# Second PV ahead of the transposes, an earlier v load, chosen PSUM tiles for the first FFN1 work, and no visit behind f0

## The chip, the cores and the metric

One core of one Trainium2 chip runs the whole kernel. The time is device microseconds (us) of an execution. An execution reads some 1.8 us more than the span of its profile (before: 417.85 us timed, 416.07 us span). Every comparison below is between fast-state runs, unless it says otherwise. "Granted clock" is the TensorE clock in the profile, 1.00 being full speed. Its records begin with the first stretch at full clock; what runs before that counts as 1.00 in the views and in the mean, whatever its speed.

## The reference

```python
scores = (1/sqrt(64)) * q @ k.T - log(448)        # q, k, v: 8 batches x 12 heads x 448 x 64
attn   = 1 / (1 + exp(-scores))                   # sigmoid, no softmax: tiles are independent
x      = (attn @ v) laid out as 3584 tokens x 768
g      = x @ w_gate                               # 768 x 1536
h      = g * sigmoid(g) * (x @ w_val)
out    = h @ w_out                                # 1536 x 768
```

## The kernel before

The work comes in quads: four heads of one batch, so 24 quads, three to a batch. A quad has 7 score tiles. Each is written by TensorE (four concurrent 64x64 products), goes through the sigmoid on ScalarE, and is used by the PV product of the quad; three PVs make one batch's input of FFN1. FFN1 of a batch is 12 tiles, f0 to f11, of 12 matmuls each: six for the gate, six for the value. In the views `st` is a loaded q or k, `c` its cast, `T` or `Tk` the transposed one, `pt` a sigmoid's output, `xT` the input of FFN1, and `s`, `t`, `hT` are the three steps from an FFN1 tile to h (sigmoid of the gate, then two products). Everything that TensorE writes goes through a ring of four PSUM tiles of two banks:

```python
ring = [psD.tile([128, 2, 512], FP32, tag=f"D{i}", name=f"ps_D{i}") for i in range(4)]
# Banked(): the next tile of the ring; Banked(at=i): a chosen one, the ring does not move on
def chunk(n, c):
    sig_tile(n, c, qk_tile(n, c))          # scores of tile c of quad n, then its sigmoid
```

The start, before FFN1 can run at full speed (GpSimd's loads, then the part of the program order that matters):

```python
    load_v(0)
    ... # casts of quad 1
    w_load("g", 0)
    load_v(1)
    w_load("v", 0)
    load_v(2)
    ...
    chunk(1, 5)
    chunk(1, 6)
    trans_pe(3)                            # 14 transposes on TensorE into one ring tile, two copies on VectorE
    for c in range(3):
        chunk(2, c)
    pv(1)
    ...
    chunk(2, 3)
    chunk(2, 4)
    # then FFN1 tiles f0..f2 of batch 0, cut up by chunk(2, 5), chunk(2, 6) and pv(2)
```

After the start, a list of units (FFN1 tiles, sums, output tiles) is run in order. A "visit" puts three or four score tiles of a later quad between two units when an estimated clock says so; the PV of the quad that is complete goes into the next visit.

```python
    for dur, fn, args in units:
        if vi < len(visits) and tcur >= vtime[vi]:
            ... # the visit
        fn(*args)
        tcur += dur
```

Tile f0 is issued in two parts (four input pairs, then two), because the last third of its input comes from the PV just ahead of it. The k and q of quads 6 and later are loaded to a staging tile by GpSimd's queue, cast there, and transposed by a DMA of SyncE.

## Time and profile before

| | before |
|---|---|
| time, median of 3 | 417.59 us (417.5 to 417.6) |
| span of the profile, mean clock | 416.1 us, 1.00 |
| TensorE busy | 403.6 us |
| first sigmoid, fourteenth sigmoid | 6.77, 18.47 us |
| second PV, FFN1, third PV | 20.52, 23.01, 27.16 us |
| first matmul of tile f3 of batch 0 | 32.65 us |
| from there to the end | 383.42 us |

The prediction below shows the main views. One that it doesn't show is the list of TensorE's waits: what waited, for what, us in total, how often, and the longest. Two of its rows belong to the change:

```profile
PE ps_D L198 <- ACT pt L246: 2.2, 3, 1.2
...
PE ps_D L294 <- DVE t L314: 0.4, 2, 0.2
```

The first is the transposes in the start. The second is the tile after f0, waiting for VectorE's read of f0, in two batches. I measure a stall differently in this document: as the time from one matmul's start to the next one's, over the median for the same pair of lines. Then these two are 0.29 us each (at 167.9 and 232.3 us). A third of 0.30 at 332.0 is inside a visit behind f0.

### The profile page before, as it was taken

The numbers are of one execution on the slowest core, as the hardware profiler recorded it, in microseconds if no ns is written. First come the engines' busy times: TensorE is split into PE (matmuls) and PEld (weight loads), VectorE is DVE, ScalarE is ACT, GpSimd is POOL, SyncE is SP. The second block draws the span as 40 slices with busy tenths as digits, with TensorE's granted clock in tenths as the row PEclk, the third lists the DMA queues.
The fourth block names the chain that finished last, engine by engine and source line by source line (L and its number), as shares of the span: only waits on it lengthen the run. The fifth ranks groups of instructions, "written<-read, shape, count | busy, mean of one in ns | idle before, by whom it ended". The sixth has DMA issues, their size and how long they took to land.

```text
span 416.1 us, 7945 instructions
## 1 busy us (share of the span) xinstructions
PE 403.6 (97%) x3194; PEld 210.7 (51%) x3194; DVE 257.2 (62%) x472; ACT 213.5 (51%) x294; POOL 94.6 (23%) x125
## 2 busy tenths in 40 slices
PE   7699999999999999999999999999999999999995
PEld 3444544445555445445565445445555545555563
DVE  3727647679855555668654555568745447588653
ACT  5966885745454745755704945745715562222000
POOL 4528063336030463110030335300000000000000
PEclk9999999999999999999999999999999999999999
DMA  8999999976779995331274998630025400000135
GB/s 254 253 253 244 226 185 236 187 184 172 189 131 241 187 195 166 71 107 24 55 190 134 201 165 191 144 57 0 2 63 137 112 2 0 2 0 2 38 80 148
DMA packets 59845, 54.39 MB, mean 131 GB/s; under 512 B 35744, under 2 KB 53280, under 8 KB 59808
## 3 DMA queue, kind: packets, MB, share of 16 engines
q0 software_dynamic: 18880, 30.94, 34.7%
q1 hardware_dynamic: 40496, 22.62, 24.9%
q8 instruction: 25, 0.41, 0.4%
q10 hardware_dynamic: 432, 0.33, 0.3%
q14 instruction: 12, 0.10, 0.1%
HBM read 47.19 MB, written 11.01 MB: 140 GB/s over the span
## 4 chain that ended last, share of the span: by engine, by line
PE 88%; ACT 5%; DVE 3%; DMA 1%; issue 1%; SPq 0%; DVEq 0%; ACTq 0%
PE ps_D L294 50%; PE ps_D L418 18%; PE ps_D L228 7%; PE ps_D L260 7%; PE ps_D L476 5%; ACT pt L246 3%; DMA st<-in_k_dram 1%; DVE t L314 1%; PE ps_D L198 1%; ACT s L312 1%; DVE S L377 1%; ACT pt L243 1%; DVE xT L269 0%; DVE hT L318 0%; DVE xT L274 0%
## 5 line engine op out<-in xcount | busy, mean ns | idle before, releaser
L246 ACT ACTIVATE pt<-ps_D,sb_t 128x896 f16<-128x896 f32 x148 | 140.3, 1011 | 82.0 <-PE ps_D L228 76.6
L294 PE MATMUL ps_D<-xT,wg 128*128 128x448 f16 x576 | 126.9, 353 | 1.1 <-ACT pt L246 0.5
L294 PE MATMUL ps_D<-xT,wv 128*128 128x448 f16 x576 | 126.5, 353 | 0.0
L314 DVE TENSOR_TENSOR t<-ps_D,s 128x448 f16<-128x448 f32 x96 | 59.8, 623 | 75.7 <-ACT s L312 75.3
L312 ACT ACTIVATE s<-ps_D 128x448 f16<-128x448 f32 x96 | 52.6, 548 | 85.2 <-PE ps_D L294 73.2
L294 PEld LDWEIGHTS <-wg 128*128 128x128 f16 x576 | 53.5, 98 | 59.2 <-issue 13.7
L294 PEld LDWEIGHTS <-wv 128*128 128x128 f16 x576 | 56.3, 98 | 52.9 <-issue 0.3
L179 POOL CAST c<-st 128x896 bf16<-128x896 f32 x41 | 38.2, 941 | 127.3 <-DMA T<-c 63.8
L318 DVE SCALAR_TENSOR_TENSOR hT<-ps_D,t 128x448 f16<-128x448 f32 x96 | 60.0, 625 | 10.0
L228 PE MATMUL ps_D<-T,T 64*64 64x448 bf16 x644 | 44.2, 357 | 1.4 <-DVE T L204 0.6
L260 PE MATMUL ps_D<-pt,v 64*64 64x448 f16 x672 | 36.0, 350 | 0.4 <-ACT pt L246 0.3
L429 DVE TENSOR_SCALAR osb<-ps_D 128x384 f32<-128x384 f32 x43 | 24.0, 558 | 19.1 <-PE ps_D L418 18.1
L418 PEld LDWEIGHTS <-S 128*128 128x128 f16 x264 | 25.8, 98 | 17.1
L418 PE MATMUL ps_D<-wT,S 128*128 128x384 f16 x198 | 34.0, 327 | 0.0
L228 PEld LDWEIGHTS <-T 64*64 64x64 bf16 x644 | 15.2, 105 | 23.8 <-issue 18.2
L269 DVE CAST xT<-ps_D 128x448 f16<-128x448 f32 x24 | 15.0, 623 | 19.9 <-PE ps_D L260 14.5
L435 DVE SCALAR_TENSOR_TENSOR osb<-ps_D,osb 128x384 f32<-128x384 f32 x33 | 18.4, 558 | 13.5 <-PE ps_D L418 13.5
L172 POOL DMA_DIRECT2D v<-in_v_dram x24 | 17.5, 730 | 39.9 <-PE ps_D L228 35.3
L274 DVE CAST xT<-ps_D 64x448 f16<-64x448 f32 x42 | 26.1, 621 | 0.7
L260 PEld LDWEIGHTS <-v 64*64 64x64 f16 x672 | 19.8, 107 | 13.1 <-issue 1.1
L418 PEld LDWEIGHTS <-hT 128*128 128x128 f16 x198 | 18.9, 98 | 14.2 <-issue 2.1
L476 PE MATMUL ps_D<-wo,hT 128*128 128x384 f16 x144 | 24.2, 327 | 0.3 <-DVE osb L489 0.3
(45 smaller groups left out, 211.6 us busy)
## 6 DMA issues: line engine op xcount, KB each, us to landing
out_dram<-osb SPq DMA_DIRECT2D x52, 192.0 KB, 2.9
st<-in_q_dram POOLq DMA_DIRECT2D x20, 448.0 KB, 5.0
st<-in_k_dram POOLq DMA_DIRECT2D x20, 448.0 KB, 6.4
v<-in_v_dram POOLq DMA_DIRECT2D x24, 224.0 KB, 7.7
wg<-in_moe_w_gate_dram POOLq DMA_DIRECT2D x4, 576.0 KB, 11.9
wv<-in_moe_w_val_dram POOLq DMA_DIRECT2D x4, 576.0 KB, 13.3
wo<-in_moe_w_out_dram POOLq DMA_DIRECT2D x4, 576.0 KB, 10.0
st<-in_q_dram SPq DMA_DIRECT2D x3, 448.0 KB, 7.1
```

Of the source, the lines that this page charges most:

```text
L179: eng.tensor_copy(out=t.rearrange("p c h d -> p h c d"), in_=st.rearrange("p h (c d) -> p h c d", c=C))
L228: nc.tensor.matmul(out=sc[w * 64:(w + 1) * 64, h2, :S], lhsT=kt[r, w * 64:(w + 1) * 64], rhs=qt[r, :, w * 64:(w + 1) * 64], start=True, st ...
L246: nc.scalar.activation(out=pt, in_=sc[:, :, :S], func=SIGM, bias=sb_t, scale=qkscale)
L260: nc.tensor.matmul(out=P[g:g + 64, h2, :S], lhsT=vt[r, h2, c * D:(c + 1) * D], rhs=pt[r, h2, :], start=(c == 0), stop=(c == C - 1),)
L274: done = [nc.vector.tensor_copy(out=o, in_=i) for o, i in halves[how:]]
L294: nc.tensor.matmul(out=D.t[:, i, :S], lhsT=w16[f // FW][:, pr, cs], rhs=xT[(b, pr)], start=(pr == 0), stop=(pr == NP - 1),),
L312: D.read(nc.scalar.activation(out=s16, in_=D.t[:, 0, :S], func=SIGM), 0)
L314: D.read(nc.vector.tensor_tensor(out=t1, in0=D.t[:, 0, :S], in1=s16, op=MULT), 0)
L318: nc.vector.scalar_tensor_tensor(out=hT[(b // 2, f)][:, b % 2, :], in0=D.t[:, 1, :S], scalar=HSC, in1=t1, op0=MULT, op1=MULT),
L418: nc.tensor.matmul(out=D.t[:, bank, :hw], lhsT=l, rhs=B_(i), start=(first and i == 0), stop=(i == HF - 1), skip_group_check=True,),
L429: nc.vector.tensor_scalar(out=o, in0=D.t[:, bank, :hw], scalar1=HREC, scalar2=None, op0=MULT), bank
L476: nc.tensor.matmul(out=D.t[:, half, :hw], lhsT=h[:, m * 128:(m + 1) * 128], rhs=wo16[f // FW][:, f % FW, half * hw:(half + 1) * hw], start ...
```

## The change

The intent is to fill the holes in the start and to take three stalls out of the rest. It has four parts. (1) v of quad 1 is loaded ahead of the first weights. (2) Two score tiles of quad 2 and the second PV go ahead of the transposes of quad 3. (3) The last scores stand together, so FFN1's early tiles are interrupted only once, and they use chosen PSUM tiles. (4) No visit goes right behind f0.

```diff
@@ loads
+    load_v(1)
     w_load("g", 0)
-    load_v(1)
@@ start
     chunk(1, 6)
+    chunk(2, 0)
+    chunk(2, 1)
+    pv(1)
+    chunk(2, 2)
     trans_pe(3)
-    for c in range(3):
-        chunk(2, c)
-    pv(1)
@@ early FFN1
     chunk(2, 4)
+    chunk(2, 5)
     k0 = ring_at[0] % 4
-    early = [Banked("f")]
-    ffn1_mm(early[0], 0, 0, range(2))
-    chunk(2, 5)
-    ffn1_mm(early[0], 0, 0, range(2, NP - 2))
-    chunk(2, 6)
-    early.append(Banked("f"))
-    ffn1_mm(early[1], 0, 1, range(NP - 2))
-    pv(2, how=2, at=(k0 + 1) % 4)
-    early.append(Banked("f", at=(k0 + 2) % 4))
+    chunk(2, 6, at=(k0 + 1) % 4)
+    early = [Banked("f", at=(k0 + i) % 4) for i in (0, 2)]
+    ffn1_mm(early[0], 0, 0, range(NP - 2))
+    ffn1_mm(early[1], 0, 1, range(2))
+    pv(2, how=2, at=(k0 + 3) % 4)
+    ffn1_mm(early[1], 0, 1, range(2, NP - 2))
+    early.append(Banked("f", at=(k0 + 1) % 4))
     ... # e2 and the ends of all three: as before
-    ring_order[:] = [(k0 + 1 - i) % 4 for i in range(4)]
+    ring_order[:] = [(k0 + i) % 4 for i in (3, 0, 2, 1)]
@@ visits
-        if vi < len(visits) and tcur >= vtime[vi]:
+        if vi < len(visits) and tcur >= vtime[vi] and not (was is ffn1 and was_args[1] == 0):
```

(`chunk` and `qk_tile` take `at` and hand it on; `was` and `was_args` are the unit just run.)

More of the change, by code (lines that the diff above doesn't have):

```diff
@@ L219, with qk_tile @@
     xT = {}
-    def qk_tile(n, c):
-        sd = Banked()
+    def qk_tile(n, c, at=None):
+        sd = Banked(at=at)
         sc = sd.t
@@ L593, in ready, with chunk @@
         trans(n)
-    def chunk(n, c):
-        sig_tile(n, c, qk_tile(n, c))
+    def chunk(n, c, at=None):
+        sig_tile(n, c, qk_tile(n, c, at))
     chunk(0, 0)
@@ L688 @@
     pend = []
+    was, was_args = ffn1, (0, 2)
     for dur, fn, args in units:
-        if vi < len(visits) and tcur >= vtime[vi]:
+        if vi < len(visits) and tcur >= vtime[vi] and not (was is ffn1 and was_args[1] == 0):
             group = visits[vi]
@@ L709 @@
         fn(*args)
+        was, was_args = fn, args
         tcur += dur
```

## The prediction

> **What bounds the kernel now.** I read the page's summary and chain first, then a table of stretches, then the timeline wherever that table shows TensorE short of full.
>
> ```profile
> PE 403.6 (97%) x3194; PEld 210.7 (51%) x3194; DVE 257.2 (62%) x472; ACT 213.5 (51%) x294; POOL 94.6 (23%) x125
> PE 88%; ACT 5%; DVE 3%; DMA 1%; issue 1%; SPq 0%; DVEq 0%; ACTq 0%
> ```
>
> TensorE is busy for 403.6 of 416.1 us and makes up 88% of the chain that ended last. All that any reordering can win is the 12.5 us in which it is idle, plus what its tile-mode switches cost. Two per cent of 417.59 us is 8.35 us. The stretches (start:end, length, then busy time and count of PE, PEld, DVE, ACT, POOL, then clock, DMA share, GB/s) say where the idle time lies:
>
> ```profile
> 10.00:15.00 5.00, 3.65 (x60) 2.10 (x58) 2.71 (x6) 5.00 (x7) 5.00 (x7) 1.00 1.15 312
> 15.00:20.00 5.00, 3.25 (x51) 2.19 (x51) 4.73 (x9) 4.55 (x6) 0.61 (x2) 1.00 1.30 206
> 20.00:25.00 5.00, 4.28 (x60) 2.24 (x50) 2.34 (x4) 4.84 (x6) 2.15 (x4) 1.00 1.30 203
> 25.00:30.00 5.00, 5.00 (x50) 2.29 (x49) 0.62 (x1) 2.19 (x3) 1.26 (x2) 1.00 1.21 283
> 300.00:360.00 60.00, 59.87 (x444) 31.88 (x443) 33.37 (x58) 24.95 (x35) 0.00 (x0) 1.00 0.23 55
> 360.00:420.00 60.00, 51.63 (x295) 28.56 (x292) 35.88 (x73) 6.52 (x12) 0.00 (x0) 0.98 0.18 47
> ```
>
> Of the idle time, 4.5 us is the tail (416.1 − 360 − 51.63), which the change leaves alone, and some 3 us lies before 10 us, also untouched. From 10 to 25 us it is 1.35 + 1.75 + 0.72 = 3.8 us. There ScalarE is full (5.00 and 4.55 of 5 us): it computes the 21 sigmoid tiles of quads 0 to 2. The timeline of that place (start, length, engine, line, operation):
>
> ```profile
> 17.97 1.16 DVE L179 CAST c<-st 128x896 bf16<-128x896 f32 x2
> 18.64 0.93 PEld L198 LDWEIGHTS <-c 128*128 128x128 bf16 x14 [1.58 <-DVE c L179]
> 18.64 1.10 PE L198 MATMUL ps_D<-idn,c 128*128 128x128 bf16 x14 [1.15 <-ACT pt L246]
> 19.31 1.16 DVE L204 COPY T<-ps_D 128x896 bf16<-128x896 bf16 x2 [0.19 <-PE ps_D L198]
> ```
>
> The transposes of quad 3 begin at 18.64 because VectorE's cast of its q, the first of the two in the 1.16 us row, ends at 18.59; the weight load names it. The matmul's row names ScalarE, whose tile had been released at 17.76: a wait put down to the wrong engine. Everything behind them in program order waits too: the first scores of quad 2, so the sigmoids, and the second PV, which takes the transposes' PSUM tile and waits for their two copies.
>
> ```profile
> 6.77 12.78 ACT L246 ACTIVATE pt<-ps_D,sb_t 128x896 f16<-128x896 f32 x14 [1.36 <-PE ps_D L228]
> 20.16 6.57 ACT L246 ACTIVATE pt<-ps_D,sb_t 128x896 f16<-128x896 f32 x7 [0.61 <-ACT pt L246]
> 20.36 1.25 PEld L260 LDWEIGHTS <-v 64*64 64x64 f16 x28 [0.36 <-DMA v<-in_v_dram]
> ```
>
> Fourteen sigmoids run without a break, then comes a hole, then the other seven, the last of which ends at 26.73. The third row is a second lock on the same PV: its v only landed at 20.32, behind the first gate weights in GpSimd's queue.
>
> Later, single stalls of 0.2 to 0.4 us remain. The clearest is behind tile f0 of a batch:
>
> ```profile
> 166.69 0.54 ACT L312 ACTIVATE s<-ps_D 128x448 f16<-128x448 f32 x1 [2.43 <-PE ps_D L294]
> 166.96 0.76 PE L228 MATMUL ps_D<-T,T 64*64 64x448 bf16 x12
> 167.27 0.62 DVE L314 TENSOR_TENSOR t<-ps_D,s 128x448 f16<-128x448 f32 x1 [1.62 <-ACT s L312]
> 167.95 0.73 PE L294 MATMUL ps_D<-xT,wg 128*128 128x448 f16 x3 [0.22 <-DVE t L314]
> ```
>
> A visit with three score tiles takes the other three PSUM tiles, so the next FFN1 tile needs f0's own. f0 is split (pairs 0 to 3, then 4 and 5), so its gate half is done only two matmuls before its end, its sigmoid starts late, and TensorE waits for VectorE's read.
>
> **What the Trainium skill says.** "TensorE: Matmul & The Clock Gate", section Back-to-back issue gap, gives N/2.4 + 2.5 ns, 189 ns for 448 columns; here the median from start to start within FFN1 is 0.189 us, in agreement. "TensorEngine Tiling (Array Packing)", Key Properties: changing the tiling mode drains TensorE. In the trace a 64x64 score group to an FFN1 matmul takes 0.282 us from start to start, against 0.179 from scores to PV and 0.189 within FFN1: a switch costs about 0.1 us. "PSUM — Partial Sum Buffer", Summary: guard by bank, evacuate promptly; here every stall above ends with some engine's last read of a ring tile or with an operand's arrival. "DMA: Bandwidth & Descriptors", Queues, rings and completion order: an engine consumes a ring's descriptors in order. The landing records agree: first gate weights 19.39, v of quad 1 20.32, first value weights 23.21, v of quad 2 24.41, in the order of issue.
>
> **The change, part by part.** No arithmetic is added or removed; I replay the start with the durations of before. Sigmoids follow each other at 0.890 us and each frees its tile about 1.06 us after its start; a PV takes 1.17 us to its last group; the xT casts are 3 x 0.64 us; two T copies 1.16 us.
>
> 1. *v of quad 1 ahead of the weights.* It is 224 KB and takes 1 us of the queue, so it should land near 17.5 and the gate weights near 20.3; the value weights stay at 23.2. FFN1 starts after that, so this costs nothing and removes the lock at 20.36.
>
> 2. *PV 1 and quad 2's scores ahead of the transposes.* Scores (2,0) take the tile of (1,4), free at 17.76, and (2,1) that of the second transposes, free at 18.05. So sigmoid 15 follows sigmoid 14 at 18.47 + 0.89 = 19.36 instead of 20.16, 0.80 us earlier, and a second hole of 0.21 us ahead of the last sigmoid closes as well. Sigmoid 21 ends at 25.71 instead of 26.73. PV 1 starts at 18.70 (tile of (1,5) free at 18.65) instead of 20.52 and its last inputs come at 19.55, ahead of its last group at 19.87. The xT casts end at 22.17, the T copies (tile free at 20.37, PE 0.74 us) at 23.36. Scores (2,3) to (2,6) start at 21.35, 22.22, 22.43 and 23.09, each ahead of its sigmoid (22.03, 22.92, 23.81, 24.70).
>
> 3. *Last scores together, early FFN1 in chosen tiles.* Before, the run of early FFN1 was cut by (2,5), (2,6) and PV 2: six switches; now by PV 2 alone: two. FFN1 starts at 23.09 + 0.28 = 23.37, later than the 23.01 of before. Twelve matmuls, 2.27 us, then PV 2 at 25.74 (before 27.16); its last group, 1.17 later, finds sigmoid 21 done. Then 0.28 for the switch and 24 matmuls of 0.189: 25.74 + 1.17 + 0.28 + 4.54 = 31.73 for the first matmul of tile f3. PV 2's copies end at 29.01, ahead of the need at 29.46, so the 0.25 us hole at 30.58 goes too. The same sum for before is 27.16 + 1.17 + 0.28 + 20 x 0.189 + 0.25 = 32.64 (trace: 32.65). **Gain 0.92 us.** From there on the order of tiles in the ring is the same relative to their users.
>
> 4. *No visit behind f0.* Four visits move back by an FFN1 tile (in batches 3, 4, 5 and 6, with one more pushed along). Three of them show a stall in starts over the usual gap: 0.29 us at 167.9, 0.29 at 232.3, 0.30 at 332.0; the one in batch 5 shows none. Behind f1 the gate half ends six matmuls before the end, as behind every other tile, so I take all three as gone: **0.88 us.**
>
> Sum 0.92 + 0.88 = 1.80 us on the path; 417.59 − 1.80 = 415.8 us.
>
> **Rivals.** *Weights become the bound:* wg and wv of tiles f6 to f8 landed at 39.79 and 42.64, and tile f6 starts at 43.05, its value half 1.13 later at 44.18. A second earlier leaves 0.6 us, so it should hold; were it to bind, the front gain alone would shrink by some tenths, 416.1. *v of quad 1 is late all the same,* or the T copies behind the xT casts hold the first early tile: FFN1 would start near 24 and the front gain would be 0.3, 416.4. *ScalarE keeps its holes* because scores (2,3) and (2,4) have only 0.3 us to spare: 0.2 to 0.4 us lost, 416.1. *The stall behind f0 only moves,* as the moved visits now lie close to the following ones and ScalarE has up to seven sigmoids in a row, which at 50.84 and 55.10 costs 0.15 and 0.18 us: gain 0.5 instead of 0.88, 416.2. A larger gain is hard to find: ScalarE's 21 sigmoids at 0.89 us from 6.77 on set a floor of 25.7 for PV 2's inputs, and PV 2 already starts there.
>
> **Range and chances.** The misses that I can name cost 0.3 to 0.6 us each and would rarely fall together; runs agree within 0.1 us here. So 415.8, from 415.0 to 416.7. Neither 8 us of gain nor of loss has a source in the profile: within 2% at 0.98.
>
> **What would show it.** Sigmoids in one row without a hole from 6.8 to 25.7; no v wait at PV 1; PV 2 near 25.7; tile f3 starting near 31.7; TensorE full from 23.4 on; no wait on VectorE's t or ScalarE's pt at f1 of batches 3, 4 and 6; the stall of 0.42 us at the first output tile (104.3) still there, unmoved in kind. I am wrong if f3 starts no earlier than 32.3, if tile f6 waits for weights, or if other waits appear behind the moved visits.

## The result

| | before | after |
|---|---|---|
| time, median of 6 of the same rounds | 417.6 us (417.2 to 417.69) | 417.04 us (416.27 to 418.73) |
| span of the profile, mean clock | 416.1 us, 1.00 | 415.2 us, 0.996 |
| first, fourteenth sigmoid | 6.77, 18.47 | 6.66, 18.68 |
| second PV, FFN1, third PV | 20.52, 23.01, 27.16 | 18.91, 23.72, 26.09 |
| first matmul of f3 | 32.65 | 32.10 |
| f3 to the end | 383.42 | 383.12 |

The ratio is 0.9989, with a 95% interval of 0.997 to 1.0009: the same within 2%. A ratio here is the mean time of one kernel's fast runs over that of the other's of the same rounds, so it is not quite the ratio of the medians that are quoted. The prediction was 415.8 us with a range of 415.0 to 416.7, and 417.04 is outside it. The kernel gained about a third of what I had summed.

The page's summary line and chain of the changed kernel:

```profile
PE 404.5 (97%) x3194; PEld 210.9 (51%) x3194; DVE 257.1 (62%) x472; ACT 213.4 (51%) x294; POOL 95.0 (23%) x125
PE 87%; ACT 5%; DVE 4%; issue 2%; DMA 1%; SPq 0%; DVEq 0%; ACTq 0%
```

TensorE is busy 0.9 us longer with the same 3194 matmuls. Something made them slower. The table of stretches says where (start:end, length, then PE, PEld, DVE, ACT, POOL busy, then clock, DMA share, GB/s):

```profile
10.00:15.00 5.00, 4.47 (x62) 2.94 (x62) 2.62 (x5) 5.00 (x6) 5.00 (x7) 0.78 1.15 296
15.00:20.00 5.00, 3.75 (x66) 2.25 (x61) 4.09 (x7) 5.00 (x7) 1.19 (x2) 1.00 1.31 207
20.00:25.00 5.00, 4.07 (x53) 2.21 (x43) 3.02 (x5) 5.00 (x7) 2.16 (x3) 1.00 1.30 203
...
360.00:420.00 60.00, 50.76 (x290) 28.11 (x288) 35.11 (x71) 6.53 (x12) 0.00 (x0) 0.98 0.18 47
```

ScalarE is now full in all three stretches of the start, as intended. But the first stretch has a clock of 0.78. The busy 4.47 us there is slow work and no gain. Cutting at the places where the granted clock changes shows a whole step:

```profile
5.36:8.78 3.42, 1.65 (x25) 0.89 (x28) 1.67 (x4) 1.98 (x3) 1.41 (x2) 1.00 1.03 369
8.78:12.19 3.41, 3.25 (x34) 1.81 (x22) 2.04 (x4) 3.32 (x4) 3.41 (x6) 0.50 1.13 318
```

For one stretch of 3.41 us the clock is half. ScalarE's timeline (start, length, engine, line, operation; in brackets the idle time before):

```profile
6.66 1.91 ACT L246 ACTIVATE pt<-ps_D,sb_t 128x896 f16<-128x896 f32 x2 [1.22 <-PE ps_D L228]
8.87 17.18 ACT L246 ACTIVATE pt<-ps_D,sb_t 128x896 f16<-128x896 f32 x19 [0.31 <-PE ps_D L228]
```

The hole behind the fourteenth sigmoid is gone: nineteen run in one row to the end of the start. A new hole of 0.31 us stands ahead of the third sigmoid. It looks like the half clock, but in this trace it isn't. The chain that ended last (start, length, what) has it in both kernels; before:

```profile
1.76 4.79 DMA st<-in_k_dram
...
8.67 4.61 ACT pt L246 x5
```

and after:

```profile
1.76 4.99 DMA st<-in_k_dram
...
8.87 4.61 ACT pt L246 x5
```

From the landing of this k (the second load of quad 0's k) to the third sigmoid it takes 8.67 − 6.55 = 2.12 us before and 8.87 − 6.75 = 2.12 after, so the 0.20 us are the load's. From the third sigmoid to the fourteenth it takes 9.80 and 9.81 us. The half clock cost these sigmoids nothing here. The place that the change aimed at:

```profile
18.31 0.57 PE L228 MATMUL ps_D<-T,T 64*64 64x448 bf16 x8 [0.62 <-DVE T L204]
18.91 1.52 PE L260 MATMUL ps_D<-pt,v 64*64 64x448 f16 x28
...
23.41 0.38 PE L228 MATMUL ps_D<-T,T 64*64 64x448 bf16 x4 [0.32 <-ACT pt L246]
23.72 0.93 PE L294 MATMUL ps_D<-xT,wg 128*128 128x448 f16 x4
```

PV 1 runs straight behind quad 2's first scores and waits for no v. The last scores (23.41) still wait for a sigmoid to free a tile, and FFN1 starts 0.31 us after them.

In TensorE's list of waits, both rows with L294 are gone, and there is a new one behind f3:

```profile
PE ps_D L228 <- DVE hT L318: 0.2, 1, 0.2
```

(Another new row, 0.5 us of scores waiting for VectorE's cast `xT`, is that of scores (2,5) at 22.52 us. The prediction has them at 22.43, and the last scores, at 23.41, wait for a sigmoid.)

### The profile page after: what moved, and what is told of

Read it like the earlier page. It is cut to its first block, busy times and chain, and to the rows that moved or that the text cites. A ratio compares the mean times of both kernels' runs of the same rounds, so it can differ in the third digit from the quotient of the medians.

```text
span 415.2 us, 7941 instructions
## 1 busy us (share of the span) xinstructions
PE 404.5 (97%) x3194; PEld 210.9 (51%) x3194; DVE 257.1 (62%) x472; ACT 213.4 (51%) x294; POOL 95.0 (23%) x125
## 4 chain that ended last, share of the span: by engine, by line
PE 87%; ACT 5%; DVE 4%; issue 2%; DMA 1%; SPq 0%; DVEq 0%; ACTq 0%
PE ps_D L294 49%; PE ps_D L418 18%; PE ps_D L228 8%; PE ps_D L260 6%; PE ps_D L476 6%; ACT pt L246 4%; DVE t L314 1%; DVE hT L318 1%; DMA st<-in_k_dram 1%; DVE S L377 1%; PE ps_D L198 1%; ACT s L312 0%; ACT pt L243 0%; SPq L149 0%; DVE T L204 0%
## 5 line engine op out<-in xcount | busy, mean ns | idle before, releaser
L294 PE MATMUL ps_D<-xT,wg 128*128 128x448 f16 x576 | 126.8, 353 | 0.1
L294 PE MATMUL ps_D<-xT,wv 128*128 128x448 f16 x576 | 126.4, 352 | 0.0
L294 PEld LDWEIGHTS <-wg 128*128 128x128 f16 x576 | 53.5, 98 | 58.3 <-issue 12.4
L294 PEld LDWEIGHTS <-wv 128*128 128x128 f16 x576 | 56.4, 98 | 52.6
```

The costliest lines, as they stand in the source:

```text
L294: nc.tensor.matmul(out=D.t[:, i, :S], lhsT=w16[f // FW][:, pr, cs], rhs=xT[(b, pr)], start=(pr == 0), stop=(pr == NP - 1),),
```

## The experiments

Two yardsticks are used throughout, because they are finer than the times. The **start distance** is the time from the start of the fourteenth sigmoid to the first matmul of tile f3: 14.18 us before, 13.42 after. It leaves out what happens earlier, and it repeats: 14.18 to 14.21 us in the four traces with the old start, 13.42 to 13.44 in those with the whole new one. The other is the list of **stalls** behind f3, in starts over the usual gap. Kernels that share a chip share the runs of the kernel before. All results were correct. My theory going in was that parts 1 to 3 gave somewhat less than 0.92 us, that the rule moved stalls instead of removing them, and that the clock had taken some of the rest in the profiled execution. (For the sigmoids the trace above shows that it hadn't.) The rivals are named in the expectations.

### after_again, front_only, visits_only, spread (one chip; before there: median 417.7 us of 11)

`after_again` is the changed kernel, unchanged.

> The changed kernel once more, for its spread. Theory A (the clock gate): a quiet window of TensorE in the first 20 us lets the granted clock fall to half for one 3.4 us stretch in some executions; fast executions lie near 416.3 us with a mean clock of 0.999 to 1.000, others near 417.0 with 0.995 or 0.996. Rival B (transfers): the slow executions have a full clock and wait for weights around 42 us. Median 416.3 to 417.1.

Measured: 417.06 us (416.46 to 418.23), ratio 0.9981 (0.9967 to 0.9995). The start distance is 13.42 again, the half clock came again (fourteenth sigmoid 12.03 us after the first, mean clock 0.995), and the stalls are the same: 0.32 at 173.7, 0.38 at 238.2. So the trace of the result was typical. But the slowest execution, 418.23, had a mean clock of 0.999. Falls like this one can't be all of the spread.

`front_only` takes the rule for visits out:

```diff
-        if vi < len(visits) and tcur >= vtime[vi] and not (was is ffn1 and was_args[1] == 0):
+        if vi < len(visits) and tcur >= vtime[vi]:
```

> The changed kernel with the rule for visits taken out again, so only the start is reordered. Theory: the start is worth some 0.6 to 0.9 us and the rule for visits 0.3 us (three stalls of 0.9 us gone, two new ones of 0.7 us), so about 0.3 us above the best of the changed kernel: 416.6 to 416.9, with stalls back near 167, 231 and 331 us. Rival (the rule is worth the 0.88 us that I predicted): 417.2 or more.

Measured: 416.86 us (416.44 to 417.61), ratio 0.9975 (0.9961 to 0.9989). The trace has the three old stalls back (0.29 at 167.6, 0.29 at 231.9, 0.31 at 331.6) and not the two new ones, and f3 to the end takes 383.47 us against 383.12 and 383.07 with the rule. But by the times it is no slower than the changed kernel. That part of the expectation failed: the difference is smaller than the scatter of executions.

`visits_only` is the kernel before with the rule alone:

```diff
-        if vi < len(visits) and tcur >= vtime[vi]:
+        if vi < len(visits) and tcur >= vtime[vi] and not (was is ffn1 and was_args[1] == 0):
```

> The kernel before with the rule for visits alone. Theory: 0.2 to 0.3 us faster than before, with new stalls of 0.3 to 0.4 us in the visits near 174 and 238 us in place of those near 168 and 232. Rival (0.88 us): 416.7. And for the spread: if it comes from the reordered start, this kernel is as steady as before (0.5 us from lowest to highest).

Measured: 417.4 us (417.06 to 418.05), ratio 0.9991 (0.9978 to 1.0004). The start distance is 14.21, as before. The three old stalls are gone and the new ones are there: 0.32 at 174.0 and 0.38 at 238.5. So the new stalls come from the rule and not from the new start. Their sum is 0.70 in place of 0.88, a gain of 0.18.

`spread` asks whether the distance between visits matters. From batch 3 on, there must be two FFN1 units between one visit and the next (`gap` counts units since the last visit):

```diff
-        if vi < len(visits) and tcur >= vtime[vi] and not (was is ffn1 and was_args[1] == 0):
+        if vi < len(visits) and tcur >= vtime[vi] and not (was is ffn1 and (was_args[1] == 0 or was_args[0] > 2 and gap < 2)):
```

> The changed kernel with at least two FFN1 tiles between visits from batch 3 on. Theory: the two new stalls (0.32 and 0.38 us near 174 and 238) come from a gate's sigmoid queueing behind the three score sigmoids of the visit one tile earlier; with two tiles between they go, 0.6 to 0.7 us less than the changed kernel of the same rounds. Rival (VectorE, not ScalarE, is what is behind): no gain.

Measured: 416.34 us (415.7 to 418.14), ratio 0.9973 (0.9954 to 0.9992). Both stalls are gone. The timelines show why. Three places, first the kernel before (around the visit behind f0 of batch 4):

```profile
231.30 0.76 PE L228 MATMUL ps_D<-T,T 64*64 64x448 bf16 x12
...
235.74 0.62 DVE L318 SCALAR_TENSOR_TENSOR hT<-ps_D,t 128x448 f16<-128x448 f32 x1
...
236.41 0.57 PE L228 MATMUL ps_D<-T,T 64*64 64x448 bf16 x8
```

then the changed kernel:

```profile
232.98 0.76 PE L228 MATMUL ps_D<-T,T 64*64 64x448 bf16 x12
233.47 2.80 ACT L246 ACTIVATE pt<-ps_D,sb_t 128x896 f16<-128x896 f32 x3 [0.98 <-PE ps_D L228]
236.16 0.55 ACT L312 ACTIVATE s<-ps_D 128x448 f16<-128x448 f32 x1
237.47 0.62 DVE L318 SCALAR_TENSOR_TENSOR hT<-ps_D,t 128x448 f16<-128x448 f32 x1
238.15 0.57 PE L228 MATMUL ps_D<-T,T 64*64 64x448 bf16 x8 [0.21 <-DVE hT L318]
```

and `spread`:

```profile
233.16 2.80 ACT L246 ACTIVATE pt<-ps_D,sb_t 128x896 f16<-128x896 f32 x3 [0.98 <-PE ps_D L228]
235.64 1.30 PE L294 MATMUL ps_D<-xT,wg 128*128 128x448 f16 x6
235.84 0.55 ACT L312 ACTIVATE s<-ps_D 128x448 f16<-128x448 f32 x1
```

A visit of three score tiles gives ScalarE 2.80 us of sigmoids. The gate sigmoid of the one FFN1 tile that follows stands behind them in ScalarE's queue, VectorE's two reads of that tile stand behind the gate sigmoid, and the last scores of the next visit need that tile. From the scores of the first visit to those last scores, the chain takes 238.15 − 232.98 = 5.17 us. In the kernel before it takes 236.41 − 231.30 = 5.11 us. It is the same chain. Before, TensorE had lost 0.29 us at f0 on the way, which let the chain catch up; without that loss TensorE arrives early and waits 0.38 at the chain's end. In the other place (167 us) the kernel before had two FFN1 tiles between these visits, and the rule left one, at 173.7 the same chain. `spread` puts a second FFN1 tile (235.64) between the visits, 2.3 us of TensorE's work, and the chain no longer sets the pace.

### pv_late, tiles_old, v_late, v_late_2, v_late_3: one part of the start undone at a time

`pv_late` undoes part 2 (before on that chip: 418.3 us, as for `tiles_old` and `v_late`):

```diff
-    chunk(2, 0)
-    chunk(2, 1)
-    pv(1)
-    chunk(2, 2)
     trans_pe(3)
+    for c in range(3):
+        chunk(2, c)
+    pv(1)
```

> The changed kernel with the transposes of quad 3 ahead of quad 2's scores and the second PV again. Theory: they wait for VectorE's casts as before, sigmoid 15 starts 0.8 us late, and tile f3 starts 14.1 to 14.3 us after sigmoid 14 (changed kernel 13.42, before 14.18): the whole gain of the start is gone. Rival (the early FFN1 order alone carries the gain, four tile-mode switches of 0.1 us fewer): 13.7 to 13.9.

Measured: 417.32 us (417.16 to 418.48), ratio 0.9983 (0.9967 to 0.9999), start distance 14.34. ScalarE's timeline has the hole again:

```profile
20.20 6.39 ACT L246 ACTIVATE pt<-ps_D,sb_t 128x896 f16<-128x896 f32 x7 [0.88 <-ACT pt L246]
```

Without this part none of the start's gain is left. The theory held by the start distance. By the times (ratios 0.9981 and 0.999 in the changed kernel's other rounds) neither this kernel nor the next can be told from the changed one.

`tiles_old` undoes part 3, so the early FFN1 block is that of the kernel before:

```diff
-    chunk(2, 5)
-    chunk(2, 6, at=(k0 + 1) % 4)
-    early = [Banked("f", at=(k0 + i) % 4) for i in (0, 2)]
     ... # and the block of the kernel before in its place, with its ring_order
```

> The changed kernel with the early FFN1 tiles and the last two score tiles in the order and the PSUM tiles of before. Theory: scores (2,5) take the tile of quad 3's transposes, whose copies now come after the xT casts and end near 23.5, so FFN1 and the last scores slip: f3 13.9 to 14.1 us after sigmoid 14. Rival (order of these tiles does not matter once the sigmoids run without a hole): 13.4 to 13.6.

Measured: 417.1 us (416.63 to 417.74), ratio 0.9972 (0.9957 to 0.9988), start distance 13.64. Part 3 is worth 0.22 us. I had expected more; the rival was nearer. FFN1 itself starts at 4.17 us behind the fourteenth sigmoid here and at 5.04 in the changed kernel, so part 3 gives up an early start for fewer interruptions, and the two almost cancel.

`v_late` and `v_late_2` undo part 1, `v_late_3` is the same kernel on a third chip:

```diff
-    load_v(1)
     w_load("g", 0)
+    load_v(1)
```

> The changed kernel with v of quad 1 behind the gate weights again. Theory: each of the three steps at the start is needed. v lands near 20.3 us, so PV 1 starts near 20.4 instead of 18.8, sigmoid 17 starts some 0.8 late, and tile f3 starts 1.0 to 1.3 us later than in the changed kernel, counted from sigmoid 14: 14.4 to 14.7 us against 13.42. Rival (v is hidden anyway because PV 1 isn't what the sigmoids wait for): below 13.7.

> The changed kernel with v of quad 1 behind the gate weights, one more look, because in the first one the clock fell to half and sigmoid 14 came 0.7 us late, so that v (19.7 us) was hardly waited for. Theory: in an execution with a full clock, v lands 1.1 to 1.8 us after sigmoid 14 starts and tile f3 starts 0.4 to 1.2 us later after sigmoid 14 than 13.42. Rival (there is slack behind PV 1): 13.4 to 13.5 again.

> v of quad 1 behind the gate weights, a third look, wanted with a full clock at the start: then sigmoid 14 starts near 18.5 us, v lands 1.1 to 1.8 us later, and tile f3 starts 13.8 to 14.6 us after sigmoid 14. Rival (slack behind PV 1, as in the two looks so far): 13.4 to 13.5.

The first two settled nothing. Their times were 418.0 (416.71 to 419.11) and 417.26 us, and both traces show a start distance of 13.42, as if the part did nothing. But in both the first stretch at full clock began only at about 14 us (16 scores from 8.74 us on take 1.71 us in `v_late`, 0.95 in `before`), and the fourteenth sigmoid started at 19.2 and 19.3. v landed at 19.74 and 19.79. PV 1 started 0.6 us behind that sigmoid instead of 0.23, and the start distance did not suffer, so a v that is late by 0.4 us is absorbed. `v_late_3` had the full clock there: 419.19 us (419.03 and 419.35), ratio 1.003 (1.001 to 1.005), start distance 16.03. Its timeline of TensorE:

```profile
20.08 2.81 PE L260 MATMUL ps_D<-pt,v 64*64 64x448 f16 x28 [1.40 <-DMA v<-in_v_dram]
```

and its stretches, cut where the clock changes:

```profile
16.74:20.15 3.41, 1.40 (x24) 0.43 (x25) 2.36 (x5) 3.41 (x5) 0.63 (x1) 1.00 1.30 204
20.15:23.56 3.41, 3.41 (x36) 1.59 (x37) 0.55 (x1) 1.38 (x3) 0.90 (x3) 0.50 1.30 203
```

PV 1 waits 1.40 us for v. The stretch in which it waits has TensorE busy for only 1.40 of 3.41 us, and in the next one the clock is half, so that the PV itself takes 2.81 us instead of 1.52. Together these are 1.40 + 1.29 = 2.69, about the measured 16.03 − 13.42 = 2.61. So part 1 is needed, and in this trace it is worth more than the wait that it removes.

### before_look, before_look_2: does the clock fall in the kernel before, too?

Both are the kernel before, unchanged.

> The kernel before, one more trace. Theory: its executions are hit by the late transposes too, so about one trace in three shows k of quad 6 landing after 62 us and a stall near 63 us, shorter than in the changed kernel by the lead that the start gives (0.77 us), and a span of 416.5 to 417.3; otherwise 416.0 and no stall there.

> The kernel before, one more trace: with chance one in three, k of quad 6 after 62 us and a stall of up to 0.7 us near 63 us at a span of 416.5 to 417.3; otherwise 415.9 to 416.1, f3 14.2 us after sigmoid 14 and stalls near 168, 232 and 332 us as in the two traces so far.

Measured: 417.44 us and 417.92 us (ratios 0.9988 and 1.0), start distances 14.20 and 14.18, the three old stalls in both. In the first the clock held. In the second it fell to half from 8.39 to 11.80 us, and the fourteenth sigmoid came 12.34 us after the first in place of 11.70 (0.21 of it by the clock, see below). The stretch ahead of that fall:

```profile
4.97:8.39 3.42, 1.55 (x25) 0.83 (x22) 1.68 (x4) 2.28 (x3) 1.27 (x3) 1.00 1.00 362
```

So the half clock is no property of the change. Both kernels have the same thin work from 5 to 10 us. The clock changes on a raster of 3.41 us (each of its records lasts that or a multiple, but for the last) whose place differs from one execution to the next: the first stretch at full clock begins between 3.91 and 7.06 us in 17 of the 20 traces, and at about 14 in three. What makes it fall is not settled. Cut at the raster, the stretch ahead of a fall had 1.40 (`v_late_3`), 1.55 (here), 1.65 (the result), 2.00 (`after_again`, 4.66 to 8.07 us) and 2.06 us (`front_only`, 4.54 to 7.96) of TensorE's work, but stretches with 1.89 (`pv_late`, 14.88 to 18.29) and 1.98 us (`spread_3`, 8.75 to 12.16) were not followed by one. So thin work goes with the falls, and the busy time alone doesn't say which thin stretch is followed by one.

### sums_after: another stall that the prediction had left alone

`spread`, and VectorE's last sums of the first output group go behind the first output tile:

```diff
-            o_units += ts[:4] + [(FU2, ffn2, (pb, 0))] + ts[4:] + [(FU2, ffn2, (pb, 3))]
+            o_units = o_units[1:] + o_units[:1] + ts[:4] + [(FU2, ffn2, (pb, 0))] + ts[4:] + [(FU2, ffn2, (pb, 3))]
```

> The kernel with two tiles between visits, and in addition the last sums of batches 0 and 1 behind the first output tile instead of ahead of it. Theory: the stall at the second output tile near 103.7 us (0.34 us, on VectorE's copy, which stands behind those sums) goes; 0.2 to 0.4 us faster than without. Rival: the sums then stand ahead of the next copies and the stall only moves: no gain.

Measured: 416.68 us (415.79 to 418.15), ratio 0.9964 (0.9944 to 0.9984), on the second chip. The stall near 104 us is gone in the trace. But the trace had a new one, 0.64 us at 63, with a follow-on of 0.93 at 80, and by the times it can't be told from `spread`. The stall near 104 drifts anyway: 0.42, 0.13 and none in three traces of the kernel before.

### after_3, spread_2, spread_3: the stall at 63 us

The slow executions with a mean clock of 0.999 (418.73 of the result, 418.23 of `after_again`) were still without a cause, so both kernels were profiled again.

> The changed kernel a third time, in the rounds of its two successors: 0.3 to 0.8 us slower than the kernel with two tiles between visits; 417.0, and a difference from the kernel before of 0.7 to 1.1 us, as the two traced sums say (0.77 at the start, 0.3 from the rule for visits).

> The kernel with two tiles between visits once more, as the partner of the next. Theory B2 (late transposes): its executions fall into a group near 416.3 us and single ones over 417.6, in which the transposed k of quad 6 lands near 63 us instead of 60. Median 416.2 to 416.9.

> The partner of the kernel with held-back loads, unchanged: some executions near 416.3, others near 418; median 416.3 to 417.6.

Measured: `after_3` 417.47 us (416.83 to 418.55), ratio 0.999; `spread_2` 417.56 (415.71 to 418.1), ratio 0.9981; `spread_3` 416.83 (415.57 to 417.56), ratio 0.9974. The profiled execution of `after_3` was one of the slow ones, 418.55 us with a mean clock of 1.000. TensorE's timeline:

```profile
64.05 0.57 PE L228 MATMUL ps_D<-T,T 64*64 64x448 bf16 x8 [1.33 <-DMA T<-c]
```

It waits for the k of quad 6, which a DMA transposes. The landing times of that transfer, from the traces' records:

| traces | issued | landed | took |
|---|---|---|---|
| 13 traces: before (3), after (2), others | 52.5 to 53.4 | 59.5 to 61.4 | 6.8 to 8.4 |
| sums_after, spread_2, v_late, after_3 | 53.0 to 53.8 | 63.04, 63.55, 63.97, 64.00 | 10.0 to 10.9 |

All 17 traces have the same loads here. In four of them the transposed k is late (and so is the q transposed just ahead of it: 56.4 to 56.9 us against 54.1 to 55.0), the stall is 0.64 to 1.40 us, and a follow-on of up to 0.9 comes near 80 us. The profiled executions concerned are longer than the other profiled ones of the same kernel: 418.55 against 416.99 and 417.01 for the changed kernel, 417.04 against 416.28 and 415.57 for `spread`. All four have the new start (4 of 12), and none of the five traces with the old one, or with the old place of the second PV, has it. That is too few to say that the change causes it.

### q6_early, k_first, k6_first: moving that transfer

All three build on `spread`. `q6_early` loads q and k of quad 6 earlier, ahead of the last gate and value weights:

```diff
     load_v(5)
+    load(6, 0, G)
+    load(6, 1, G)
     w_load("g", 3)
...
-        (4, 0): ((fetch, 6),),
-        (4, 4): ((ready, 6),),
+        (4, 0): ((load_v, 6), (ready, 6)),
```

> The same kernel with q and k of quad 6 loaded ahead of the last gate and value weights, so that their transposes are issued some 3 us sooner. Theory B2: the transposed k lands well before 60 us in every execution, the stall at 62 to 63 us (0.57 and 0.68 us in the two traces that show it) can't occur, and the executions over 417.6 become rare; the fast ones are as before, so the median falls by 0.1 to 0.4 us. Rival (the clock gate alone makes the spread): as wide a spread as its partner.

Measured: 423.51 us (417.62 to 425.6), with three runs slow, the profiled one among them; ratio of the fast ones 1.0053 (1.001 to 1.0097). A miss. The transpose was issued at 47.7 and landed at 69.25, with the last value weights (landing at 52.3) and the loads of quad 7 (issued from 47.2 on) beside it, and TensorE waited 6.8 us. Issuing it earlier made it later.

`k_first` does the opposite. GpSimd copies one column of the transposed k to a scrap tile before it issues the next loads, so those can't start while the transpose runs:

```diff
+    def landed(n):
+        nc.gpsimd.tensor_copy(out=seen, in_=qT[(n, 1, C - 1)][:, :1])
...
-        (5, 4): ((fetch, 7), (w_out, 0)),
+        (5, 4): ((landed, 6), (fetch, 7), (w_out, 0)),
-        (6, 4): ((fetch, 8), (w_out, 2)),
+        (6, 4): ((landed, 7), (fetch, 8), (w_out, 2)),
```

> The kernel with two tiles between visits, in which the loads of quads 7 and 8 are issued only once the transposed k of the quad before has landed (a one-column copy on GpSimd waits for it). Theory B3: the transposed k is late because it shares the 16 engines with those loads; alone it lands near 56.5 us (issued at 53, 3 us as for q) instead of 60 to 64, so the stall at 62 to 64 us never occurs and the executions lie within 1 us, median near 416.2, 0.5 to 1 us below its partner's. Rival: the lateness belongs to the queue of transposes itself or to slower transfers in general, and k lands after 60 us all the same; or the loads held back make quad 7 or 8 late (stall near 77 or 80 us).

Measured: 423.55 us (418.04 to 428.23), ratio 1.0089 (1.0046 to 1.0132), the profiled run slow. The transposed k landed at 57.16, as expected, 4.5 us after its issue. But holding the loads twice made quad 8's k late, for a wait of 5.6 us at 100 us.

`k6_first` keeps only the first of the two holds, `landed(6)`.

> Two tiles between visits, and only the loads of quad 7 held back until the transposed k of quad 6 has landed; those of quad 8 go as before, since holding them back too cost 5.7 us at 100 us. Theory B3: k of quad 6 lands near 57.3 us, as in the trace with both held back, quad 7's near 76, ahead of its need near 77; no stall at 63 us, executions within about 1 us, ratio to the kernel before 0.996 to 0.9965 against 0.9973 to 0.9981 without. Rival: the delay is passed on to quad 7 or 8 in some executions, a stall of 1 us or more near 77 or 92 us, ratio 0.998 or worse.

Measured: 416.15 us, all five runs from 415.94 to 416.58; ratio 0.9961 (0.9947 to 0.9974). The transposed k lands at 56.44, 4.0 us after its issue, and the scores that need it run at once:

```profile
62.50 0.57 PE L228 MATMUL ps_D<-T,T 64*64 64x448 bf16 x8
```

One wait of 0.4 us for a transposed operand is left at 77.4 us. This is the lowest median, and the only set of five or more runs without one above 416.6. It is below the kernel before of its own rounds (417.97 us) in every run. It was not run beside the changed kernel on one chip, but its slowest run is below the changed kernel's median in each of that kernel's rounds (417.04, 417.06, 417.47). Its interval overlaps those of `spread`, so that the hold gains over `spread` is likely but not shown.

## Why the prediction was wrong

The mechanism of the start was right, the effect of the rule was wrong, and the scatter was underestimated. The profiles account for it (us, plus is a gain; "predicted" is the prediction's own term):

| term | predicted | measured in the profiles |
|---|---|---|
| start distance (steps 1 to 3) | 0.92 | 14.18 − 13.42 = 0.76 |
| rule for visits (step 4) | 0.88 | 0.88 − 0.70 = 0.18 |
| first to fourteenth sigmoid | 0 | 11.70 − 12.02 = −0.32 |
| first sigmoid | 0 | 6.77 − 6.66 = 0.11 |
| stall near 104 us gone, by drift | 0 | 0.42 |
| stall near 96 us, by drift | 0 | −0.23 |
| remainder | 0 | −0.06 |
| sum | 1.80 | 416.07 − 415.21 = 0.86 |

The two rows of sigmoids together make the fourteenth 0.21 us later. As shown above, 0.20 of it is the later landing of quad 0's k.

**Steps 1 and 2, right.** v was no longer awaited at PV 1, the fifteenth sigmoid followed the fourteenth by 0.89 us as computed, and PV 1 started 0.24 us behind the fourteenth (computed 0.23). v landed at 15.81 us and the gate weights at 19.91, both earlier than estimated (17.5 and 20.3). `pv_late` and `v_late_3` show that each of the two parts is needed.

**Step 3, right in kind, too large by 0.16.** Relative to the fourteenth sigmoid, the prediction had FFN1 at 4.90 us and the trace has it at 5.04; from there to f3 it had 8.36 and the trace has 8.38. So nearly all of the miss lies ahead of FFN1. The failing term is "each frees its tile about 1.06 us after its start". In an unbroken row the sigmoids of the trace start 0.890 us apart, but each takes some 8 ns longer than the one before: 1.007 us for the first of the row, 1.085 for the fourteenth, 1.117 for the eighteenth, 1.142 for the last. The tile that the last scores need is freed by the eighteenth, which starts 4 x 0.89 = 3.56 us behind the fourteenth, at 22.24. It ends at 23.36 and the scores start at 23.41, so 1.17 us behind its start where I had taken 1.06: 0.11 lost. From these scores to FFN1 it takes 0.31 and not 0.28: 0.03. Together that is the 0.14. The longer row that I wanted is what made this grow, since the old hole used to reset it (1.007 again for the fifteenth, before).

**Step 4, wrong.** The sentence that failed is "I take all three as gone: 0.88 us". All three went, but two came back as 0.32 and 0.38. I had named this as a rival ("the stall behind f0 only moves") with a gain of 0.5, and even that was too kind: 0.18. I looked only at the wait that ended last, not at what stood behind it. The chain of 5.11 us through ScalarE and VectorE could be read from the profile before, beside TensorE's work in the same stretch without the stall, 5.11 − 0.29 = 4.82. Taking 0.29 off TensorE's side had to uncover it. `visits_only` shows that the rule alone does this, and `spread` that one more FFN1 tile between the visits ends it.

**The range, too narrow.** With the two corrected terms the sum is 0.94 and the time 417.59 − 0.94 = 416.65, only just inside the range. The rest of the way to the median of 417.04 I put down to scatter, which I had set at 0.1 us from three runs of the kernel before. Its sources shown in traces are four. Quad 0's second load of k lands between 5.72 and 6.88 us, in both kernels. A half clock that begins at 7.96 to 8.39 us costs 0.21: from that landing to the third sigmoid it takes 2.33 us in `after_again`, `front_only` and `before_look_2`, against 2.12 in the result, where it began later (8.78), and in `before` and `after_3`, which had none. A full clock that only comes at 14 us (`v_late`, `v_late_2`, `k_first`) puts the fourteenth sigmoid at 19.2 to 19.3 us, against 18.3 to 18.8 in the other traces. And the late transposed k costs 0.64 to 1.40 us, plus its follow-on. In its three sets of rounds the changed kernel's median is 0.56, 0.64 and 0.68 us below that of the kernel before, so part of the gap to 0.94 may belong to the new start. The two fastest executions of the result, 416.27 and 416.29 us with clocks of 1.000 and 0.999, show what the changed kernel does when little of this strikes. That it didn't is only inferred; they were not profiled.

**Rivals that did not happen.** No FFN1 tile waits for weights in the list of waits, and ScalarE kept no hole from scores (2,3) and (2,4).

**Left open.** Whether the old start escapes the late k by its timing or only by luck of five traces; what makes the sigmoid longer in a row; what makes the clock fall; and whether a kernel can do anything about where the clock's raster lies. That 418.73 and 418.23 had a late k is likely but not shown, as only the profiled executions have records. A late full clock is a rival that their mean clock doesn't exclude: `v_late` had both, at 418.52 us, and its mean clock reads 1.000.

## What to carry to other kernels

Before counting a stall as gained, take it out of the timeline by hand and follow the next chain of the other engines over the same stretch: where it is longer than the first engine's work without the stall, the stall will come back. When visits of a second kind of work are interleaved, the distance between them is a quantity of its own, as each one fills another engine's queue for microseconds. Before blaming a low clock, measure the distance between two events of the chain with it and without: in the result's trace it was the same 2.12 us. And three runs that agree within 0.1 us don't bound the scatter; gains of tenths need traces of several executions, and a thin stretch of matmuls or a transfer with little slack is worth treating as a cost even if the profile at hand escaped it.

## What the Trainium skill lacked or had wrong

- "TensorE: Matmul & The Clock Gate", section Why this matters for your kernels, asks for no idle gaps of more than about 3 us to keep the clock. Here the clock fell with no gap above 0.7 us (after) and 1.40 us (`v_late_3`). The length of the stretch (3.41 us) and the factor of a half agree with the page's Part 1. Its section on a second failure mode says that many short idles can do it, but gives no figure, and the runs here don't yield one: falls came after stretches with 1.40 to 2.06 us of work, and stretches with 1.89 and 1.98 us passed without.
- "DMA: Bandwidth & Descriptors", Rules for kernel authors, says that a transpose next to ordinary DMAs needs nothing. It speaks of corrupted data, and for the data it agrees: all results were correct. Of the time it says nothing, and the pages that give a transpose's bandwidth don't say what other loads do to it. The same DMA transpose took 4.0 to 4.5 us with the next loads held back, 6.8 to 8.4 with the usual ones, 10.0 to 10.9 in four traces with the same loads, and 21.5 with other weights and loads beside it (`q6_early`).
- "ScalarE: Activation LUTs", section What ACT_TABLE_LOAD costs, gives (N + 335)/1.2 ns for such an ACTIVATE, 1026 ns for 896 columns, and an overlap of about 93 ns back to back. The first of a row took 1007 ns, in near agreement, but the starts are 889 to 890 ns apart, so the overlap is 118 ns, and each one in a row takes some 8 ns longer to its end (1.142 us for the last), which the page doesn't mention and which moves the release of its PSUM tile.
